# A pre-norm attention and feed-forward block on one Trainium2 core: a different hand-fixed order for the same 1,426 entries

## The chip, the cores and the metric

The kernel runs on one core of one Trainium2 chip. The metric is device microseconds of one execution. Six parts of the core matter: TensorE (PE, with its weight loads shown as PEld), VectorE (DVE), ScalarE (ACT), GpSimd (POOL), SyncE (SP), whose queue issues most of the DMAs, and the DMA engines that carry them.

## The reference

One block with two halves and residual additions. Every operand is bfloat16, with 2,048 tokens, width 640, 32 heads of 20 and a hidden width of 1,728.

```
h  = x + A(layernorm(x))          h2 = h + B(layernorm(h))

A: q, k, v = x @ wq, x @ wk, x @ wv
   for each of 4 segments of 512 tokens:
       a_dot = softmax(q k^T / sqrt(20) + causal mask) v          (within the segment)
       a_mem = (phi(q) M) / (phi(q) z + 1e-6)                     (memory of earlier segments)
       out   = sigmoid(beta) * a_mem + (1 - sigmoid(beta)) * a_dot
       M, z += phi(k)^T v, sum phi(k)       phi(t) = t + 1 if t > 0 else exp(t)
   A = out @ wo
B: silu(x @ w1) @ w2
```

## The kernel before

The program is cut into named tasks, and a list called `ORDER` (line 356) puts every one of them in a row. An entry is `name/engine:slots`. The letter after the slash picks the engine where a task may run on more than one: A is ScalarE, D VectorE, G GpSimd, and S the SyncE queue. The numbers are the buffers that the task takes, for most of them one of the eight PSUM banks. `schedule` (line 287) walks the list once, fixes engine and buffers of each task, and every engine then gets its instructions in the order of the list. A tracker adds the semaphore waits that the buffers need. So an engine never overtakes: an instruction that waits holds all that stands behind it on that engine, DMA issues among them.

The work of a segment `s` of four blocks of 128 tokens, with the lines that the profile names:

- `n1_st`, `n1_r`, `n1_ap`: statistics (L743, L746), reciprocal root (L754 to L764) and scaling (L770) of the first layer norm. `n1_tr` transposes a block by DMA into `xT` (L799); the four blocks of segment 0 go through TensorE instead (`n1_tp`, L779; `n1_te`, L791, L792). `n2_` is the same for the second norm, into `hT`.
- `re_wq`, `re_wk` (L693, L695): the weights of the queries and keys are rearranged once.
- `v` (L828) and `ve` (L842, L843): values, and their eviction from PSUM.
- `pr` (L867, L872) and `qe` (ScalarE L883 or VectorE L884): queries and keys of a chunk of heads, and the eviction. In segment 0 each is cut into token halves x and y.
- `ex` (ScalarE, L890), `pha` (L897), `phb` (L903): phi of queries and keys.
- `vt` (L915) and `vp` (L928): DMAs that copy the heads which don't fit into the first five groups from one place of SBUF to another, twelve for each segment. Groups 5 to 7 of the scores can't start before all twelve `vt` have landed.
- `qk` (TensorE, L965) makes the scores of a group of four heads in four PSUM banks, `e` (ScalarE, L977) takes their exponential, either for four banks at once (a `+` in the name) or for two and two, and `mk` (GpSimd, L988) masks a diagonal block.
- `av` (L1009, L1093), `oe` (L1022, L1024, L1111), `tn` (L1039, L1043, L1124), `nm` (L1057 to L1063, L1136, L1138), `ad` (L1071): attention output, transposed back, normalised and added to the part from the memory.
- `kt`, `kg`, `kh`, `mz`, `ma`, `mb`: the memory of the next segment (transpose L1208, gather L1199, matmul L1226, sums L1238 to L1250).
- `ot` (DMA transpose, L1265), `wo` (L1273), `rs` (L1281): output projection and first residual.
- `h1` (L1302, L1308), `th` (ScalarE tanh, L1317), `s` (L1323), `h2` (L1350), `o` (L1363), `out` (L1368): the feed-forward half and the store. The last block's `h2` and `o` are cut into columns of 320, 192 and 128.
- `zf0` (L649) and `lsc` (L638 on) are small constants made from beta; `fill` (L620) are matmuls on zeros that keep TensorE busy: thirty at the start and two at the end of the list.

Segments overlap freely: the first half of one stands among the second half of the segment before it.

Of the kernel before, what the change touches and what calls it, by code (L numbers as in the profile page):

```python
# [370 lines left out]
e0ya+:4 w_w1_2 ve12/D av4x:4 oe4x/D:0 mz00:5 ma00/A:2,5 qk1ya0:0 e1ya2:0 tn2x:6 nm2x:0 av6x:7 oe6x/D:1 e1ya0 tn4x:6
nm4x:1 qk2ya0:2 kvz e2ya2:1 tn6x:7 mm3 nm6x:2 n1_tr4 v10:0 n1_st11:2 e2ya0 qk0y20:4 e0y2+:6 w_w1_3 w_w1_1 mk0y2_0
kg00/G:0 mk0y2_256 n1_tr7 v13:2 n1_r11/G qk3ya0:4 e3ya0:3 ve10/D n1_st9:6 n1_r9/D pha041:2 ex031:2 mm6 ve13/D ot1:0
wo1:0 n1_st8:3 e3ya2 ot0 ex011:0 wo0:2 rs1 n2_st1:0 mk0y1_384 w_w1_4 phb011 qk4ya0:4 e4ya0:2 n2_r1/D kg02/G e4ya2 rs0
# [11 lines left out]
mz02:6 pha101:1 vt13/S mk8b_384 th0_0_0:0 e9b2 mk9a_0 mk9b_0 mk8e_256 h1_0_9_0:7 th0_9_0:1 s0_0_0 ma02/D:0,4,6,7
qk10a0:0 e10a0:3 mzc2 h1_0_13_0:6 h2_0_0:4 e10a2 w_w2_4 ot3 h2_0_1 mk9b_384 mk10a_0 phb101 n1_r10/D pha111:2 vt19/S
mzc0 mb00:0,0 w_w2_3/S s0_9_0 n1_ap11:2 pha100:0 phb100 th0_13_0:0 s0_13_0 ex131:0 phb131 pha110:0 n1_ap10:1 vt12/S
qk10b0:0 e10b+:6 epsg1 av8:7 oe8/D:0 n1_tr8:0 av9:6 oe9/D:1 n1_tr9 ex110:0 phb110 vt18/S vt110/S h2_0_2 mk10b_0
mk10b_384 qk10e0:0 e10e2:2 e10e0 n1_tr11 h2_0_3 ex121:0 h2_1_0:6 o0 kt13:0 qk11a0:2 pha121:0 phb121 wo3:0 rs3 n2_st3:3  # L390
mk10e_0 mk10e_256 h2_1_1 e11a+:4 mk11a_0 vt14/S qk11b0:2 kg13/G:0 ex130:1 tn8:0 e11b+:5 h2_1_2 vt11/S h2_1_3 pha140:0
nm8:1,1 o1 kh13/G n2_r3/G ex111:2 phb111 mm1 n2_ap3:2 mk11b_0 mk11b_384 pha130:0 vt16/S mzc1 vt111/S ot2 qk12a0:2
e12a+:0 ex140:0 mzc3 mb01:0,0 wo2:0 rs2 av10:7 oe10/D:0 phb140 ad8:0 qk12b0:2 e12b0:3 mzc5 kt12:1 mz10:0 ma10 e12b2
mk12b_0 kg12/D n1_tr10 pr220:6 phb130 vt15/S vt17/S qk13a0:0 e13a+:1 mk13a_0 qe220/D:0 vp13/S:0 tn9:4 vp19/S v20:6
nm9:2,0 ve20/D:0 kt11:0 qk12e0:0 e12e+:6 vp18/S av11:4 n2_st2:4 v21:6 n2_r2/D qk13b0:0 vp15/S oe11/D:1 pr211:5 e13b+:4
# [10 lines left out]
ot4 pr230:5 pha240:0 phb210 qe230/D v22:6 ve22/D ex230:0 ot5 out1/S h1_0_13_1:4 th0_13_1:0 qk17b0:0 e17b2:3
h1_0_11_1:5 th0_11_1:1 vt29/S pha231:1 phb231 phb211 e17b0 wo6:6 mk16e_256 s0_13_1 s0_11_1 qk18b0:2 e18b2:6 mk17b_0
e18b0 mk18b_0 rs6 n2_st6:3 ex220:2 av16:0 oe16/D:1 wo7:6 rs7 n2_r6/D qk17a0:2 wo4:0 vt28/S e17a+:0 h1_0_9_1:7
th0_9_1:0 ex240:1 kg10/G vt27/S n2_st7:0 mk18b_384 vt21/S mk17b_384 vt211/S h1_0_3_1:6 mk17a_0 rs4 th0_3_1:1 n2_st4:2
s0_9_1 qk18e0:2 e18e0:1 n2_r4/D wo5:0 s0_3_1 vt23/S h1_0_2_1:7 e18e2 mk18e_0 phb240 rs5 th0_2_1:0 s0_2_1 h1_0_1_1:6  # L410
th0_1_1:1 vt24/S s0_1_1 qk18a0:2 e18a0:2 vt25/S av17:1 oe17/A:0 kt23:1 x12/S h2_2_0:6 h2_2_1 n2_ap6:1 n2_st5:6
n2_tr6:0 n2_r7/G mk18e_256 n2_ap7:3 n2_tr7 phb220 vt22/S e18a2 qk19b0:0 pha230:0 phb230 vp21/S:0 e19b0:4 tn17:4
nm17:3,1 n2_ap4:1 n2_tr4 pha200:0 h2_2_2 e19b2 h2_2_3 mk18a_0 n2_r5/G qk19a0:0 h2_3_0:4 h2_3_1 e19a2:0 o2 ad17:0
vp22/S e19a0 n2_ap5:3 n2_tr5 out2/S mk19a_0 vp24/S ex200:0 kh14/D av18:6 oe18/D:0 vt210/A phb200 qk20b0:0 e20b+:3
h2_3_2 mk19b_0 h2_3_3 o3 vp25/S ex201:1 kg14/G mz12:7 mb10:0,0 tn18:1 nm18:3,0 mk19b_384 av19:0 h1_1_10_0:6 oe19/A:0
# [1011 lines left out]
```

## Time and profile before

| | |
|---|---|
| median of 3 runs | 296.61 us (296.48 to 296.85) |
| span of the profiled execution | 296.3 us |
| TensorE, matmuls | 282.1 us busy, 2,968 in the profile |
| VectorE | 222.2 us busy |
| ScalarE | 217.3 us busy |
| GpSimd | 140.0 us busy |
| granted TensorE clock | 1.000 over the whole span |

The page of the profile has one row for each engine, the span in 40 slices, the DMA queues, the chain of work that ended last, and the costliest groups of instructions. Busy time of TensorE has the fill and drain of its pipeline in it, so a short wait can hide inside it. A row of a group tells the number of instructions, their busy time together, the mean of one in ns, and the idle time of the engine just before them with what ended it. A row of the timeline tells start, length, engine, line, what is written and read, and in brackets the idle time before it.

### The profile page before, as it was taken

The page shows a single profiled execution, that of the slowest core. Times are in us where ns is not written, and L with a number is a line of the kernel's source. Part 1 is how long each engine was busy: PE and PEld are TensorE (multiplying, and loading weights), DVE is VectorE, ACT ScalarE, POOL GpSimd, SP SyncE. Part 2 cuts the span into 40 slices and gives each one's busy share as a digit, 9 for nine tenths or more (in the row PEclk, how much of TensorE's full clock was granted, in tenths as well). Part 3 has the DMA queues.
Part 4 walks back from the last instruction along what each step waited for, and adds up shares of the span by engine and source line. Part 5 has one row for each costly group of instructions (what it writes and reads, how often), then busy time and mean ns, then how long its engine had stood idle before and what let it go on. Part 6 is the DMA issues. An engine that isn't in the chain of part 4 may idle for free.

```text
span 296.3 us, 7415 instructions
## 1 busy us (share of the span) xinstructions
PE 282.1 (95%) x2968; PEld 167.6 (57%) x2991; DVE 222.2 (75%) x506; ACT 217.3 (73%) x266; POOL 140.0 (47%) x257
## 2 busy tenths in 40 slices
PE   7897889999999999999999999999999999999997
PEld 5675445555665455566643545465665457764575
DVE  3897799778979779899698967759967688626522
ACT  4884989999999899998879999788759750014400
POOL 6237735645566477646526646455476620200000
PEclk9999999999999999999999999999999999999999
DMA  7956973803953221255433400144171023220002
GB/s 243 367 173 105 173 133 71 221 18 75 189 94 74 53 60 22 40 109 106 104 96 61 66 1 2 27 76 87 22 99 32 0 61 74 68 67 25 22 22 91
DMA packets 49922, 25.40 MB, mean 86 GB/s; under 512 B 39504, under 2 KB 48048, under 8 KB 49888
## 3 DMA queue, kind: packets, MB, share of 16 engines
q1 hardware_dynamic: 47804, 22.69, 36.2%
q10 hardware_dynamic: 2084, 2.23, 2.4%
q8 instruction: 24, 0.39, 0.5%
q14 instruction: 10, 0.08, 0.1%
HBM read 10.41 MB, written 2.62 MB: 44 GB/s over the span
## 4 chain that ended last, share of the span: by engine, by line
PE 78%; DVE 8%; DMA 6%; issue 2%; ACT 2%; SPq 1%; POOL 1%; DVEq 0%; ACTq 0%
PE ps_all L1350 19%; PE ps_all L1308 17%; PE ps_all L867 12%; PE ps_all L965 7%; PE ps_all L1273 6%; PE ps_all L828 5%; PE ps_all L1009 5%; DMA x_tok<-in_A_x_dram 3%; DMA xT<-xn_rot 2%; ACT PT L977 2%; PE ps_all L1039 1%; DVE stt L743 1%; PE ps_all L1093 1%; DMA w_sb<-w_sb 1%; PE ps_all L1226 1%
## 5 line engine op out<-in xcount | busy, mean ns | idle before, releaser
L977 ACT ACTIVATE PT<-ps_all 128x1024 bf16<-128x1024 f32 (+1 forms) x120 | 153.2, 1310 | 16.9 <-PE ps_all L965 15.7
L988 POOL TENSOR_SCALAR_AFFINE_SELECT PT<-PT 128x512 bf16<-128x512 bf16 x128 | 81.6, 648 | 59.2 <-ACT PT L977 56.9
L1350 PE MATMUL ps_all<-w_sb,sT 128*128 128x320 bf16 (+2 forms) x462 | 64.9, 295 | 0.0
L1308 PE MATMUL ps_all<-hT,w_sb 128*128 128x512 bf16 (+1 forms) x315 | 61.0, 336 | 1.2 <-issue 0.6
L1317 ACT ACTIVATE th<-ps_all 128x512 f32<-128x512 f32 (+2 forms) x70 | 34.1, 505 | 35.3 <-PE ps_all L1308 31.2
L1350 PEld LDWEIGHTS ps_all<-w_sb,sT 128*128 128x128 bf16 x462 | 43.2, 98 | 18.3 <-issue 1.8
L1323 DVE SCALAR_TENSOR_TENSOR sT<-th,ps_all 128x512 bf16<-128x512 f32 (+2 forms) x70 | 37.9, 561 | 17.8 <-ACT th L1317 16.9
L1308 PEld LDWEIGHTS ps_all<-hT,w_sb 128*128 128x128 bf16 x325 | 29.9, 98 | 25.3 <-issue 3.5
L764 POOL TENSOR_TENSOR rst<-rst,eps_c 128x1 f32<-128x1 f32 x32 | 18.3, 576 | 24.4 <-DVE rst L758 23.1
L743 DVE BATCH_NORM_STATS2 stt<-x_tok 128x6 f32<-128x320 bf16 x62 | 27.2, 481 | 1.1 <-DMA x_tok<-in_A_x_dram 0.7
L1363 DVE SCALAR_TENSOR_TENSOR x_tok<-ps_all,x_tok 128x640 bf16<-128x640 f32 (+3 forms) x18 | 13.3, 745 | 16.7 <-PE ps_all L1350 16.6
L1071 POOL TENSOR_TENSOR otok<-on 128x320 bf16<-128x320 bf16 x24 | 19.0, 797 | 11.7 <-DVE on L1063 11.7
L1273 PE MATMUL ps_all<-wo_sb,oT 128*128 128x320 bf16 x160 | 23.8, 299 | 0.0
L884 DVE CAST QK<-ps_all 128x512 bf16<-128x512 f32 x23 | 15.7, 688 | 9.1 <-PE ps_all L867 8.9
L1063 DVE TENSOR_TENSOR on<-ps_all,rd 128x640 bf16<-128x640 f32 x24 | 19.8, 824 | 0.9
L828 PE MATMUL ps_all<-wv_sb,xT 128*128 128x320 bf16 x120 | 18.3, 299 | 1.1 <-DMA xT<-xn_rot 0.9
L1273 PEld LDWEIGHTS ps_all<-wo_sb,oT 128*128 128x128 bf16 x160 | 15.0, 98 | 7.2 <-issue 1.8
L867 PE MATMUL ps_all<-xT,wkr 128*128 128x512 bf16 x67 | 16.9, 379 | 1.2 <-issue 0.8
L867 PE MATMUL ps_all<-xT,wqr 128*128 128x512 bf16 x70 | 17.3, 380 | 0.4 <-issue 0.2
L1009 PE MATMUL ps_all<-PT,Vx 128*32 128x512 bf16 (+3 forms) x384 | 16.4, 301 | 0.1
L843 DVE CAST Vx<-ps_all 128x640 bf16<-128x640 f32 x15 | 12.3, 818 | 5.4 <-PE ps_all L828 5.3
L770 DVE TENSOR_SCALAR xn_rot<-x_tok,mvt,rst 128x640 bf16<-128x640 bf16 x32 | 14.9, 475 | 1.7 <-POOL rst L764 1.0
(106 smaller groups left out, 337.4 us busy)
## 6 DMA issues: line engine op xcount, KB each, us to landing
w_sb<-in_B_w_dram SPq DMA_DIRECT2D x5, 432.0 KB, 6.3
w_sb<-in_B_w_dram SPq DMA_DIRECT2D x3, 480.0 KB, 4.6
x_tok<-in_A_x_dram SPq DMA_DIRECT2D x2, 640.0 KB, 9.7
out_dram<-x_tok ACTq DMA_DIRECT2D x8, 160.0 KB, 1.8
out_dram<-x_tok SPq DMA_DIRECT2D x7, 160.0 KB, 1.9
x_tok<-in_A_x_dram SPq DMA_DIRECT2D x3, 320.0 KB, 3.4
QKV<-QK SPq DMA_DIRECT2D x12, 72.0 KB
wo_sb<-in_A_wo_dram SPq DMA_DIRECT2D x1, 800.0 KB, 10.4
```

The lines of the kernel that those rows point to most:

```text
L743: T.add(DV, lambda e, hh=hh: e.bn_stats(out=stt[:, s, 6 * hh:6 * hh + 6], in_=xb[:, 320 * hh:320 * hh + 320]), reads=R((xa, xsub)), writes ...
L828: fns.append(lambda e, c=c, hh=hh: e.matmul(bank(ps, hh)[:, 0:320], lhsT=xT_[:, c, 128 * i:128 * i + 128], rhs=wv_sb[:, c, 320 * hh:320 * ...
L867: fns = [lambda e, kc=kc: e.matmul(bank(ps)[:, lo:hi], lhsT=wt[:, kc, c, :], rhs=xT_[:, kc, lo:hi], start=(kc == 0), stop=(kc == NC - 1)) ...
L965: fns.append(lambda e, j=j, o=o, r=r, q0=q0, q1=q1, qa=qa, ka=ka: e.matmul(ps_all[:, o:o + q1 - q0], lhsT=ka[32 * r:32 * r + DH, 128 * j:1 ...
L977: T.add(AC, lambda e: e.activation(out=pt[:, pta.slot, q0:q0 + nq, 0:width], in_=sc3[:, b0:b0 + nq, 0:width], func=ACT.Exp, scale=SCALE), ...
L988: T.add(PO, lambda e: e.affine_select(out=v, in_=v, pattern=[[0, 4], [1, 128]], compare_op=ALU.is_ge, fill=0.0, base=0, channel_multiplier ...
L1009: fns.append(lambda e, j=j, r=r, h=h, pa=pa, pt=pt, co=co, q0=q0, ji=ji: e.matmul(bank(po)[32 * r:32 * r + 32, q0:hi], lhsT=Vx[:, vx.slot, ...
L1273: fns.append(lambda e, c=c, hh=hh: e.matmul(bank(ps, hh)[:, 0:320], lhsT=oT[:, c, 128 * i:128 * i + 128], rhs=wo_sb[:, c, 320 * hh:320 * h ...
L1308: fns = [lambda e, c=c: e.matmul(bank(ps)[:, lo:hi], lhsT=w1_sb[:, c, 128 * f:128 * f + 128], rhs=hT[:, c, lo:hi], start=(c == 0), stop=(c ...
L1317: T.add(AC, lambda e: e.activation(out=th[:, tha.slot, lo:hi], in_=bank(ps)[:, lo:hi], func=ACT.Tanh, scale=0.5), reads=R((ps, [0])), writ ...
L1323: T.add(DV, lambda e: e.scalar_tensor_tensor(out=sT[:, f, lo:hi], in0=th[:, tha.slot, lo:hi], scalar=1.0, in1=bank(ps)[:, lo:hi], op0=ALU. ...
L1350: fns.append(lambda e, f=f, t0=t0, fr=fr, hh=hh, n=n: e.matmul(bank(pa, hh)[:, 0:n], lhsT=sT[:, f, t0:t0 + 128], rhs=w2_sb[:, fr, c0 + 320 ...
```

## The change

Only the list is another one. The 1,426 names are the same, and so are the tasks themselves and the sizes of the buffers. What differs is the order from the second line on, the PSUM banks and other slots, and the engine of some tasks that have a choice:

- 12 tasks go from VectorE to ScalarE (`re_wq1`, `qe000y`, `qe001y`, `qe010y`, `qe011y`, `ve01`, `oe11`, `qe211`, `qe301`, `qe330`, `ve33`, `oe26`), and 6 the other way (`qe041y`, `qe101`, `qe200`, `qe310`, `qe320`, `oe22`).
- 29 DMAs go from the SyncE queue to ScalarE's, among them 13 `vt` and 11 `vp`, and 13 go back. ScalarE issues 37 DMAs instead of 21.
- Sixteen small tasks (`n1_r`, `n2_r`, `kg`, `kh`) go from VectorE to GpSimd and nine the other way.
- The two `fill` matmuls stand in the middle of segment 3 (before `tn24`) instead of behind the last matmul.
- In the last block the columns are finished in another order: 128, 320, 192 instead of 320, 192, 128.

Of the diff, the lines that matter below:

```
-re_wq1/D:0 pr010x:4 re_wq4/A re_wq2/D pr020x:2 qe020x/A:0 qe010x/A:0 re_wq3/D re_wq0/D pr000x:5 pr040x:6 w_k1
...
-qe040y/A vt02/S:0 vt011/S vt05/S vt08/S n1_st5:1 qk0x30:0 vt04/S mk0x1_0 mk0x1_256 n1_st4:5 n1_r5/G n1_ap5:1 e0x3+:0
-n1_ap6:2 pr000y:4 qe000y/D lsc0 vt07/A pr021y:6 qe021y/D pr001y:5 qe001y/D pr011y:7 ex021:0 qe011y/D pr020y:1 n1_r4/D
-mk0x3_0 qe020y/D mk0x3_256 vt010/A pr010y:6 qe010y/D vt00/A vt03/A vt06/S v03:2 ve03/D:0 ex001:1 mk0x3_384 mk0x2_0
-v00:4 ve00/D qk0y10:0 e0y12:5 mk0x1_384 pha021:1 pha001:2 v01:6 e0y10 mk0y1_0 mk0x2_256 vt09/S phb021 vt01/S qk4x10:2
...
-n2_ap1:0 n2_st0:0 pr101:0 qe101/A:0 av0y:1 qk0y30:2 e0y3+:0 w_w2_0/S pr120:6 zf0 n2_r0/D oe0y/D:0 pr100:7 mk0y3_0
+re_wq1/A:0 re_wq0/D w_k1 x2:0,2 pr000x:4 re_wq4/A re_wq2/D pr020x:6 mm3 qe020x/A:0 re_wk2/A:0 w_wv0:0 re_wq3/D
...
+mk0x1_0 zf0 lsc0 qe030y/D zf1 qk0x30:0 e0x3+:0 pr021y:7 qe021y/D x8/S:7,8,11,9 vt011/A:0 pr000y:6 pr020y:5 n1_st5:5
+vt02/S mm2 pr001y:7 qe001y/A vt05/S mk0x1_256 qe020y/D n1_st7:4 n1_r7/G pha001:1 pr011y:0 lsc1 lsc2 pr010y:4 v03:2
+qe011y/A qe010y/A qe000y/A qk0y10:4 n1_ap7:1 v00:0 vt01/A vt03/A ve03/D:1 ex001:1 v01:2 phb001 mm1 e0y10:1 n1_r5/G
+n1_ap5:3 ve00/D vt06/A mk0x3_0 vt010/S n1_st4:4 n1_r6/G mk0x2_256 mk0x3_256 vt07/S vt04/S n1_ap6:2 v02:0 ve02/D vt00/A
+vt08/S ex021:0 e0y12 pha021:2 phb021 ve01/A mk0x1_384 mk0x3_384 ex011:2 vt09/S qk4x20:4 av2x:2 e4x2+:2 mk4x2_0
...
+e4ya0:5 e4ya2 mzc6 n2_st0:2 n2_r0/G mzc3 pr101:1 qe101/D:0 av0y:0 oe0y/D:1 qk0y30:2 pr100:6 n2_ap1:0 qe100/D e0y3+:3
...
+h2_5_0:6 vt35/S e27b2 mk26e_0 n2_st9:4 n2_r9/G kt21:1 mz21:1 ma21 mb21:0,0 kg22/D fill2:0 tn24:4 nm24:1,1 n2_st11:7
...
-h2_15_1_1 h2_15_2_1 h2_15_0_2:3 h2_15_3_1 out15_0/A o15_1 h2_15_1_2 h2_15_2_2 h2_15_3_2 o15_2 out15_2/A out15_1/S
-fill2:2
+o15_2 h2_15_1_0 h2_15_2_0 h2_15_3_0 o15_0 h2_15_0_1:5 out15_2/S h2_15_1_1 h2_15_2_1 out8/S h2_15_3_1 o15_1 out14/A
+out15_1/S out15_0/A
```

More of the change, by code (lines that the diff above doesn't have):

```diff
@@ L371 @@
[L371 to L374, printed above, removed]
-n2_ap1:0 n2_st0:0 pr101:0 qe101/A:0 av0y:1 qk0y30:2 e0y3+:0 w_w2_0/S pr120:6 zf0 n2_r0/D oe0y/D:0 pr100:7 mk0y3_0
@@ L386 @@
[L386 to L395, printed above, removed]
@@ L406 @@
[L406 to L415, printed above, removed]
```

158 lines of the change are left out of this document (90 added, 68 removed).

## The prediction

> **What bounds the kernel now.** I read the page's first part, then busy time by stage, then the waits, then the chain and the timeline where the waits point.
>
> ```profile
> PE 282.1 (95%) x2968; PEld 167.6 (57%) x2991; DVE 222.2 (75%) x506; ACT 217.3 (73%) x266; POOL 140.0 (47%) x257
> ```
>
> Over the whole span TensorE (PE) looks like the only bound. By stage it is not; the columns are the length, then PE, PEld, DVE, ACT and POOL, busy us with the instructions in brackets.
>
> ```profile
> 20.00:30.00 10.00, 8.50 (x86) 6.19 (x84) 8.22 (x20) 5.40 (x7) 5.69 (x11) 1.00 0.53 93
> 30.00:45.00 15.00, 12.63 (x195) 7.20 (x194) 12.95 (x31) 13.25 (x13) 9.28 (x17) 1.00 0.86 149
> 45.00:80.00 35.00, 33.40 (x441) 19.77 (x444) 29.45 (x76) 34.55 (x46) 19.03 (x35) 1.00 0.51 115
> 80.00:145.00 65.00, 63.93 (x724) 37.23 (x731) 56.31 (x129) 59.69 (x71) 40.17 (x72) 1.00 0.38 73
> 145.00:240.00 95.00, 93.07 (x987) 49.86 (x994) 72.22 (x151) 78.27 (x85) 53.04 (x88) 1.00 0.28 49
> ```
>
> From 20 to 45 us nobody is full: TensorE idles 1.50 + 2.37 us and ScalarE 4.60 + 1.75, each waiting for the other or for data. From 45 to 80 ScalarE is the bound (0.45 us idle in 35). From 80 on TensorE is (1.07 us idle in 65, 1.93 in 95), with ScalarE 5.3 us short of full in the 65. So a new order can win in the first 80 us and can only win small waits, or lose, behind that. How the two engines hand time to each other stands in the waits:
>
> ```profile
> ACT PT L977 <- PE ps_all L965: 15.7, 28, 1.8
> PEld ps_all L965 <- ACT PT L977: 13.2, 33, 1.8
> PE ps_all L965 <- DMA w_sb<-w_sb: 1.5, 1, 1.5
> PE ps_all L828 <- DMA xT<-xn_rot: 0.9, 1, 0.9
> ```
>
> The exponentials wait for scores, and the scores for banks that exponentials must empty. Two single waits of TensorE are for landings, and the chain of work that ended last runs through both:
>
> ```profile
> 24.60 3.73 DMA w_sb<-w_sb
> ...
> 35.73 6.91 DMA xT<-xn_rot
> ```
>
> The first is the last of the twelve `vt` copies of segment 0, the second the last transposed block of segment 1 (`n1_tr7`).
>
> **The change part by part.** The tasks are the same, so TensorE's work is the same; what can differ is its waiting, and what ScalarE, where it is full, has to do. I cost the change against the profiled execution (span 296.3 us, 0.3 below the median of 296.61) and carry the difference over to the median.
>
> *The first wait.* TensorE and ScalarE around the `vt` landing:
>
> ```profile
> 22.29 2.88 PE L828 MATMUL ps_all<-wv_sb,hT 128*128 128x320 bf16 x20
> 25.11 0.40 PE L965 MATMUL ps_all<-w_sb 20*128 20x256 bf16 x12
> 25.44 1.53 PE L828 MATMUL ps_all<-wv_sb,hT 128*128 128x320 bf16 x10
> 28.47 0.40 PE L965 MATMUL ps_all<-w_sb 20*128 20x256 bf16 x12 [1.50 <-DMA w_sb<-w_sb]
> ```
>
> ```profile
> 21.36 3.34 ACTq L915 DMA_DIRECT2D w_sb<-w_sb  x3
> 25.56 1.94 ACT L977 ACTIVATE PT<-ps_all 128x1024 bf16<-128x1024 f32 x2 [0.18 <-PE ps_all L965]
> 28.92 1.88 ACT L977 ACTIVATE PT<-ps_all 128x2048 bf16<-128x2048 f32 x1 [1.43 <-PE ps_all L965]
> ```
>
> Before, TensorE has three of the four value blocks done when it starts to wait at 26.97 and goes on at 28.47. In the new list the fourth (`v02`, half of the 2.88, so 1.4) stands ahead of the wait: it arrives at 28.4, plus 0.2 that I give to a later start of the y halves (block 2's scaling now stands behind block 3's), 28.6. Equal progress before is 28.47 + 1.4 = 29.9. When does the last copy land? Seven now go on SyncE's queue and five on ScalarE's, and ScalarE also takes the four y evictions.
>
> ```profile
> L883 ACT ACTIVATE w_sb<-ps_all 128x256 bf16<-128x256 f32 x11 | 3.7, 388 | 0.9 <-PE ps_all L867 0.9
> L890 ACT ACTIVATE ex<-w_sb 128x512 bf16<-128x512 bf16 x5 | 3.1, 626 | 3.0 <-DVE Vx L843 2.8 <-DVE w_sb L884 0.2
> L883 ACT ACTIVATE QK<-ps_all 128x512 bf16<-128x512 f32 x7 | 4.2, 600 | 0.1
> L649 ACT ACTIVATE zf<-beta_bc 128x32 f32<-128x32 bf16 x1 | 0.2, 222 | 0.0
> L915 ACTq DMA_DIRECT2D w_sb<-w_sb x4: 701/860/1617, 19.2 to 23.8; - x4
> out_dram<-x_tok ACTq DMA_DIRECT2D x8, 160.0 KB, 1.8
> ```
>
> The last y projection drains some 0.2 us after the first value block begins, so at 22.29 + 0.2, and with the 0.2 of the later start at 22.7. Behind it on ScalarE stand two evictions (0.39 each, 23.5), two issues (0.86 each, the first beside an eviction, 24.8), `ex001` (0.63, 25.4), then `e0y10` with two issues beside and behind it: the last starts at 26.3. Every one of these waits holds what is behind it, above all `ex021` and `e0y12`; they are needed only by matmuls behind the same landing. From issue to landing the chain shows 3.73 us for such a copy; the shortest row near it is a store's 1.8. That gives 28.1 to 30.0. I take 29.2, between the two, because the DMA engines are only 0.53 busy in 20:30 and five copies start on another queue: first scores at 29.2, 0.7 better than 29.9, range 1.3 better to 0.1 worse.
>
> For ScalarE the first four-bank exponential then starts at 29.2 + 0.45 = 29.65 instead of 28.92, 0.73 later, but with `ex011` (0.63) already behind it, which before stood among the full stretch. (`ex021`, `e0y12`, the eviction `ve01`, which ScalarE takes over, and `ex011` fill its time from the last issue on; if they run longer than to 29.65, the start is late by up to 0.3 more, which is in the range.) It also gets time back at the second landing:
>
> ```profile
> 41.88 1.88 ACT L977 ACTIVATE PT<-ps_all 128x2048 bf16<-128x2048 f32 x1 [0.21 <-PE ps_all L965]
> 44.59 1.02 ACT L977 ACTIVATE PT<-ps_all 128x1024 bf16<-128x1024 f32 x1 [0.84 <-PE ps_all L965]
> ```
>
> `n1_tr7` is issued behind fewer weight loads in the new list, so `v13` no longer holds the scores of group 3. They still need the banks of the exponential at 41.88, so of the 0.84 only about 0.4 goes, and the 0.21 goes too; `ex041` (0.63) fills what is left, 0.2 over. Sum at that point: +0.73 - 0.63 - 0.4 - 0.2 + 0.2 = **-0.3**, range -1.0 to +0.8.
>
> [...]
>
> *The full stretch, 45 to 80.* The order of exponentials is the same; of other work ScalarE loses `qe101` (0.60) and `zf0` (0.22, now ahead of 20 us, where it idles). With 0.45 us idle in 35 all of it counts: **-0.8**. VectorE takes `qe101` and has 5.5 us of room in that stretch; if VectorE's order is late there instead, the term is 0. The three `vt` issued on ScalarE here stand behind exponentials and cost nothing, as these rows show: the issue runs beside the exponential, and the next one starts on time.
>
> ```profile
> 143.02 1.02 ACT L977 ACTIVATE PT<-ps_all 128x1024 bf16<-128x1024 f32 x1 [0.70 <-PE ps_all L965]
> 143.03 0.75 ACTq L915 DMA_DIRECT2D QKV<-QK  x1
> 143.94 1.02 ACT L977 ACTIVATE PT<-ps_all 128x1024 bf16<-128x1024 f32 x1
> ```
>
> *80 to 145.* Here ScalarE issues fourteen copies and stores that SyncE issued before.
>
> ```profile
> L915 ACTq DMA_DIRECT2D QKV<-QK x2: 716/732/747, 143.0 to 190.4; - x2
> L928 ACTq DMA_DIRECT2D phiQv<-phiQ x3: 642/677/801, 217.3 to 221.7; - x3
> ```
>
> Singles behind an exponential are free. Four pairs are not: `vt110`, `vt111` behind an `ex` (2 x 0.73 - 0.63 = 0.83), `vp15`, `vp111` behind an eviction (2 x 0.68 - 0.60 = 0.75), `vt27`, `vt29` and `vt22`, `vt21` behind a two-bank exponential (2 x 0.73 - 1.02 = 0.44 each): 2.5 us in which the next exponential can't start. One eviction more (two come, one goes; 0.60) makes 3.1. ScalarE has 5.3 us idle here and is not the bound, so I put 0.3 on the path; the ends are 0 and 3.1. On the other side, SyncE's queue loses some 10 of these issues at 0.7 us each and its transposes get out earlier; TensorE's 1.07 us idle bounds that gain, I take 0.1. Together **+0.2**, range -1.1 to +3.1.
>
> *The rest.*
>
> ```profile
> L620 PE MATMUL ps_all<-zpad 128*128 128x256 bf16 x32 | 5.2, 333 | 1.1 <-DVE zpad L597 1.1
> 293.44 0.36 DVE L1363 SCALAR_TENSOR_TENSOR x_tok<-ps_all,x_tok 128x192 bf16<-128x192 f32 x1 [0.89 <-PE ps_all L1350]
> 293.80 0.38 PE L620 MATMUL ps_all<-zpad 128*128 128x256 bf16 x2
> 294.00 0.29 DVE L1363 SCALAR_TENSOR_TENSOR x_tok<-ps_all,x_tok 128x128 bf16<-128x128 f32 x1 [0.20 <-PE ps_all L1350]
> ```
>
> The two zero matmuls ran beside the last addition, for nothing; now they stand among TensorE's full stretch: at most 0.33, I take **+0.2**. The last piece is 192 columns instead of 128: 0.36 - 0.29 = +0.1. The order of the last `h1` can give as much back; 0. From 145 to 240 ScalarE has 16.7 us idle, which hides the four evictions it gains (it loses three): 0.
>
> *Tasks between VectorE and GpSimd.* Sixteen go one way, nine the other. What two engines' closeness costs can be seen at phi:
>
> ```profile
> L897 DVE TENSOR_SCALAR phiQ<-QK 128x512 bf16<-128x512 bf16 x15 | 5.6, 381 | 0.0
> L897 DVE TENSOR_SCALAR phiQ<-QK x15: 240/285/879, 56.3 to 205.3; 128x512 bf16<-128x512 bf16 x15
> ```
>
> The mean is 96 ns above the median, 1.4 us over fifteen instructions, all of it on an engine with 8.7 us of room in 80:145: 0 in the sum. [...]
>
> Sum: -0.3 - 0.8 + 0.2 + 0.2 = **-0.7 us**, so 295.9.
>
> **The rivals.** *More is won.* TensorE's idle time from 30 to 80 is 2.37 + 1.60 us, and its short waits for banks are hidden in busy time. If the new banks take half of that (2.0) in addition, 0.7 + 2.0 = 2.7: 293.9. For it: the waits between L965 and L977 are 61 short ones, the kind that an order decides. Against: ScalarE is full in most of it.
>
> *Nothing moves.* The copies land as late as before (+0.5 instead of -0.3) and the rest holds: -0.7 + 0.8 = +0.1, 296.7.
>
> *ScalarE's queue becomes the bound.* If the four pairs (2.5) fall where TensorE waits for the next scores' banks, the 0.3 becomes 2.5: -0.7 + 2.2 = +1.5, 298.1. It decides from about 1.0 us of unhidden issue on. For it: 92% of 80:145 is already busy on ScalarE. Against: TensorE is 98% busy there, so ScalarE works ahead of need.
>
> **How the numbers follow.** A measurement of this kernel can tell about 0.2%, 0.6 us, from no change. Forecast 0.33, more is won 0.20, nothing moves 0.20, ScalarE's queue 0.27. The forecast lies just over the line and the case above it well over: faster 0.52, same 0.20, slower 0.28. The range takes in 293.9 and 298.1 and a little of the bounds outside: 293.7 to 298.3. The forecast's own range, with its first term at either end, is 295.2 to 297.0.
>
> **What would show it.** Right: `L965 <- DMA w_sb<-w_sb` under 1 us or gone, `L828 <- DMA xT<-xn_rot` gone, the 0.84 us before the exponential near 44 us halved, and the scores of group 10 about a microsecond earlier than before. Wrong: issues of L915 and L928 on ScalarE's queue with the next L977 idle behind them and TensorE's L965 waiting for that; or a first exponential behind the landing later than 30.4.

## The result, and the profile after

The list after is slower: 305.73 us median of 4 runs (305.58 to 307.18) against 296.59 us (296.48 to 296.85), a ratio of 1.0313 with a 95% interval of 1.0287 to 1.0340. The forecast was 295.9 with a range of 293.7 to 298.3, so it was wrong in sign and in size. The profiled execution took 305.58 us with a span of 303.9. Its first page has a first sign in the line of the clock, one digit of which is not a 9 (slice 9, 60.8 to 68.4 us):

```profile
PEclk9999999959999999999999999999999999999999
```

The same stages as in the prediction; of the two numbers behind the instruction counts the first is the granted clock, the second the share of the DMA engines:

```profile
20.00:30.00 10.00, 9.47 (x103) 6.77 (x105) 8.70 (x23) 7.45 (x12) 6.86 (x16) 1.00 0.49 81
30.00:45.00 15.00, 11.13 (x188) 6.62 (x176) 11.68 (x26) 13.33 (x12) 10.80 (x18) 1.00 0.45 97
45.00:80.00 35.00, 30.49 (x370) 17.25 (x369) 23.66 (x58) 27.70 (x34) 14.01 (x28) 0.90 0.49 127
80.00:145.00 65.00, 63.20 (x748) 37.28 (x750) 54.60 (x126) 60.45 (x73) 40.16 (x75) 1.00 0.43 67
145.00:240.00 95.00, 93.16 (x982) 50.97 (x988) 71.88 (x156) 81.49 (x90) 53.20 (x92) 1.00 0.34 60
```

The loss sits in 45:80, where ScalarE was to win 0.8 us: TensorE is busy 30.49 us instead of 33.40 at a clock of 0.90, and ScalarE 27.70 instead of 34.55. From the waits of the two engines:

```profile
ACT PT L977 <- PE ps_all L965: 16.0, 31, 0.9
PE ps_all L1308 <- DMA hT<-xn_rot: 3.4, 1, 3.4
PE ps_all L965 <- DMA QKV<-QK: 0.8, 1, 0.8
```

One wait is new and long: the first product of the feed-forward half (`h1`, L1308) waits 3.4 us for `hT`, the transposed second norm. The DMA issues and the product around it, from the timeline, and how long the transpose issued at 54.68 (`n2_tr0`) took, from the answer on its line:

```profile
52.12 1.21 SPq L799 DMA_TRANSPOSE hT<-xn_rot  x1
53.37 1.26 SPq L1208 DMA_TRANSPOSE phiKt<-phiK  x1
54.68 1.28 SPq L799 DMA_TRANSPOSE hT<-xn_rot  x1
55.12 0.42 ACTq L582 DMA_DIRECT2D w_sb<-in_B_w_dram  x1
56.00 1.27 SPq L1208 DMA_TRANSPOSE phiKt<-phiK  x1
61.33 2.32 PE L1308 MATMUL ps_all<-hT,w_sb 128*128 128x256 bf16 x10 [3.39 <-DMA hT<-xn_rot]
```

```profile
L799 SPq DMA_TRANSPOSE hT<-xn_rot x1: 1277/1277/1277, 54.7 to 54.7; - x1
...
DMA to landing us min/median/max: 6.6/6.6/6.6
```

The transposes issued at 52.12 and 53.37 landed after 2.6 and 2.5 us. `n2_tr0`, third of the train, with the 640 KB load `w_w2_0` issued 0.44 us behind it on the other queue, took 6.6. And behind the wait the clock halves:

```profile
53.73:57.15 3.42, 2.93 (x59) 1.57 (x59) 2.97 (x7) 3.42 (x5) 1.15 (x2) 1.00 0.69 125
57.15:60.56 3.41, 0.78 (x4) 0.17 (x2) 0.69 (x1) 1.83 (x2) 1.91 (x3) 1.00 1.20 220
60.56:63.97 3.41, 2.64 (x18) 1.48 (x18) 0.42 (x1) 0.68 (x2) 0.00 (x0) 0.50 0.44 144
63.97:67.39 3.42, 3.42 (x26) 2.50 (x22) 2.14 (x7) 2.35 (x3) 0.00 (x0) 0.50 0.00 0
```

Two stretches of 3.41 us at exactly half clock follow one in which TensorE was busy for 0.78 us. My theory at this point: the late landing costs 3.4 us, the half clock it brings some 2.9 more, and all else about what was forecast. The rivals: the transpose is late because of its own place on the queue and not because of the load; the clock falls for another reason; ScalarE's 16 more DMA issues are what costs.

### The profile page after: what moved, and what is told of

Its sections match the earlier page's. It is cut to its first block, busy times and chain, and to the rows that moved or that the text cites. A ratio compares the mean times of both kernels' runs of the same rounds, so it can differ in the third digit from the quotient of the medians.

```text
span 303.9 us, 7408 instructions
## 1 busy us (share of the span) xinstructions
PE 285.1 (94%) x2968; PEld 169.9 (56%) x2991; DVE 218.1 (72%) x492; ACT 220.2 (72%) x273; POOL 140.5 (46%) x264
## 4 chain that ended last, share of the span: by engine, by line
PE 73%; ACT 9%; DMA 7%; DVE 6%; issue 2%; SPq 1%; POOL 1%; ACTq 1%; DVEq 0%
PE ps_all L1350 19%; PE ps_all L1308 16%; PE ps_all L867 12%; PE ps_all L965 7%; PE ps_all L1273 7%; ACT PT L977 7%; PE ps_all L1009 4%; PE ps_all L828 3%; DMA hT<-xn_rot 2%; PE ps_all L1039 1%; DMA oT<-otok 1%; DMA w_sb<-w_sb 1%; DVE stt L743 1%; DMA QKV<-QK 1%; PE ps_all L1043 1%
## 5 line engine op out<-in xcount | busy, mean ns | idle before, releaser
L988 POOL TENSOR_SCALAR_AFFINE_SELECT PT<-PT 128x512 bf16<-128x512 bf16 x128 | 81.0, 647 | 62.9 <-ACT PT L977 60.8
L1308 PE MATMUL ps_all<-hT,w_sb 128*128 128x512 bf16 (+1 forms) x316 | 62.8, 346 | 4.3 <-DMA hT<-xn_rot 3.4
L1308 PEld LDWEIGHTS ps_all<-hT,w_sb 128*128 128x128 bf16 x325 | 31.0, 101 | 30.0 <-DMA hT<-xn_rot 3.9
L884 DVE CAST QK<-ps_all 128x512 bf16<-128x512 f32 x24 | 16.4, 684 | 5.9 <-PE ps_all L867 5.6
L770 DVE TENSOR_SCALAR xn_rot<-x_tok,mvt,rst 128x640 bf16<-128x640 bf16 x32 | 17.0, 535 | 2.5 <-POOL rst L764 2.5
L1281 DVE TENSOR_TENSOR x_tok<-ps_all,x_tok 128x640 bf16<-128x640 f32 x16 | 13.1, 817 | 5.0 <-PE ps_all L1273 4.9
```

What stands on the lines that cost most here:

```text
L988: T.add(PO, lambda e: e.affine_select(out=v, in_=v, pattern=[[0, 4], [1, 128]], compare_op=ALU.is_ge, fill=0.0, base=0, channel_multiplier ...
L1308: fns = [lambda e, c=c: e.matmul(bank(ps)[:, lo:hi], lhsT=w1_sb[:, c, 128 * f:128 * f + 128], rhs=hT[:, c, lo:hi], start=(c == 0), stop=(c ...
```

## The experiments

All are edits of the list alone; seven of them add matmuls on zeros. Ratios are against the list before on the same chip. "Lag" is how much later a task starts on TensorE than in the second trace of the list before (next paragraph). Times to landing and waits are each from the one trace of a list.

**The base of comparison (`b0`).** The list before, unchanged.

> The list before, unchanged, for a second trace of it. In the runs so far time minus span is 1.7 to 1.8 us for every list, but 0.3 for the profiled execution of before against its median (296.6 and 296.3). Theory: that profiled execution was a long one of some 298 us; a new trace shows a span of 294.9 to 295.5, and where the 1 to 1.4 us lay. Rival: the span is again 296.3.

It took 296.93 us with a span of 295.2, and its trace has no wait for `xT`. Time minus span is 1.7 to 1.9 for every run of every list here. So the profiled execution of before that the prediction was worked out from was a long one (by the same 1.7 some 298.0 us); 0.34 us of its surplus lay at the wait for `xT` near 44 us. Against this second trace the lag of after grows as these rows show, first before, then after, the same tasks (scores of five stages):

```profile
46.39 0.40 PE L965 MATMUL ps_all<-w_sb 20*128 20x256 bf16 x8
54.74 0.40 PE L965 MATMUL ps_all<-w_sb 20*128 20x256 bf16 x8
59.90 0.40 PE L965 MATMUL ps_all<-w_sb 20*128 20x256 bf16 x8
118.98 0.40 PE L965 MATMUL ps_all<-QK 20*128 20x512 bf16 x4
231.37 0.40 PE L965 MATMUL ps_all<-QKV 20*128 20x512 bf16 x4
```

```profile
48.00 0.40 PE L965 MATMUL ps_all<-w_sb 20*128 20x256 bf16 x8
56.35 0.40 PE L965 MATMUL ps_all<-w_sb 20*128 20x256 bf16 x8 [0.24 <-ACT PT L977]
67.74 0.40 PE L965 MATMUL ps_all<-w_sb 20*128 20x256 bf16 x8
125.99 0.39 PE L965 MATMUL ps_all<-QK 20*128 20x512 bf16 x4
239.72 0.39 PE L965 MATMUL ps_all<-QKV 20*128 20x512 bf16 x4
```

+1.6 by 46 us, nothing more to 55, +6.2 to 60, -0.8 to 119, +1.3 to 231, and +0.3 to the end: 8.7, the difference of the spans.

**Only the load away (`e1`).**

```
-... e4y12 w_w2_0/A n2_tr0 ... qk4y20:2 e4y2+:4 ...
+... e4y12 n2_tr0 ... qk4y20:2 e4y2+:4 w_w2_0/A ...
```

> The list after, with one entry moved: the 640 KB load of w_w2_0 is issued on ScalarE's queue behind e4y2+ (some 15 us later) instead of behind e4y12; n2_tr0 is issued at about 54.7 us as before this edit. Theory (the load, issued 0.4 us behind n2_tr0, takes the DMA engines from it; TensorE idles 3.4 us for hT; the granted clock then halves for some 7 us and costs 2.9 more): n2_tr0 lands 2.6 to 4.0 us after its issue instead of 6.6, the wait of L1308 for hT is under 0.8 us, the clock stays at 1.0 in 60:70, and the time falls from 305.7 to about 299.7 (299 to 300.5). Rival 1 (the transpose is slow by itself, or because it is issued late, behind kt01): landing and wait stay, 305.7. Rival 2 (the clock falls for another reason than the idle time): the wait goes and the clock still halves, about 302.6.

1.0165 (1.0110 to 1.0220). The wait falls to 1.2 us, the transpose takes 4.4, not 2.6 to 4.0. But the time scatters with the clock: 307.38 at 0.945, 303.39 and 303.01 at 0.989, and 300.43, alone within the expected 299 to 300.5, at 1.0. In the profiled run it fell not near 60 but twice earlier:

```profile
28.89:32.30 3.41, 1.69 (x57) 1.10 (x57) 2.82 (x6) 2.14 (x2) 0.93 (x2) 1.00 0.57 117
32.30:35.71 3.41, 3.41 (x27) 1.72 (x26) 1.21 (x3) 1.88 (x1) 3.19 (x8) 0.50 0.49 95
...
39.13:42.54 3.41, 2.25 (x44) 1.28 (x45) 2.62 (x8) 3.11 (x5) 3.26 (x6) 1.00 0.54 153
42.54:45.95 3.41, 3.41 (x21) 1.56 (x19) 2.39 (x5) 2.07 (x3) 1.50 (x2) 0.50 0.36 70
```

So the part of the list ahead of 45 us, the same as in after, can halve the clock too: behind 3.41 us in which TensorE was busy 1.69, and behind 3.41 with 2.25.

**The transpose earlier (`e2`).**

```
-... n2_ap1:0 qe100/D ... phb041 qe120/D:0 n2_ap0:2 ... qe121/D kt01:1 e4y12 w_w2_0/A n2_tr0 ...
+... n2_ap1:0 n2_ap0:2 qe100/D ... phb041 qe120/D:0 ... qe121/D n2_tr0 kt01:1 e4y12 w_w2_0/A ...
```

> The list after, with n2_ap0 on VectorE moved ahead of qe100, phb041 and qe120, and n2_tr0 on SyncE's queue moved ahead of kt01; w_w2_0 stays behind e4y12 on ScalarE's queue. n2_tr0 should be issued at 53.4 us instead of 54.7. Theory (what counts is that the load comes right behind the transpose): with 1.7 us of lead instead of 0.4 most of the transpose is done when the load begins: it lands at 57.5 to 58.5, the wait is under 0.8 us, 299.7. Rival (the load behind takes the engines however the lead): landing about 1.3 us earlier, a wait of about 2 us, and the clock falls if 2 us are enough for that: 301.5 to 304.4.

300.67 us, 1.0107 (1.0073 to 1.0141), clock 1.0 in every run. `n2_tr0`, second of the train at 53.6, lands after 2.7 us and nobody waits; `kt01`, now third with the load 0.44 us behind it, takes the 6.0 instead, and TensorE waits 0.4 us for it near 61 us. The list is now 3.7 us over before instead of 9.1. What is left shows another landing further on: `PE ps_all L965 <- DMA QKV<-QK: 1.6, 1, 1.6`, the copies `vt2` near 152 us.

**Zeros in the wait (`e3`, `e12`).** `e3` puts 26 zero matmuls ahead of `h1_0_12_0`; `e12` also 8, 5 and 5 ahead of `qk4x10`, `qk1ya0`, `qk2ya0`.

```
-... av0x:3 qk4x10:4 ... av4x:6 qk1ya0:0 ... e1ya0 qk2ya0:2 ... qe141/D:0 h1_0_12_0:7 ...
+... av0x:3 fill8:1 qk4x10:4 ... av4x:6 fill5:7 qk1ya0:0 ... e1ya0 fill5:7 qk2ya0:2 ... qe141/D:0 fill26:7 h1_0_12_0:7 ...
```

> The list after, with 26 more matmuls on zeros for TensorE right ahead of h1_0_12_0, where it waits for hT; nothing of the computation is changed. By the 0.11 us that five 128x256 matmuls take each at full clock they fill some 2.9 of the 3.4 us. Theory (the clock halves because TensorE idles): the wait remains but the clock stays at 1.0 in 60:70, so that the 2.9 us of half clock go and the 3.4 us stay: about 302.8. Rival (the clock falls by itself, or the matmuls come late): no gain or a loss, 305.7 to 306.5.

308.09 us (1.0364, 1.0328 to 1.0400), no gain. The profiled run has a clock of 0.95 over its span of 306.9 us, which I can't explain: at 308.68 us it stands among the others (307.38 to 309.22), with 0.983 to 0.989. It settles little by itself, hence `e12`:

> The list after, with 8, 5 and 5 matmuls on zeros ahead of qk4x10, qk1ya0 and qk2ya0 and 26 ahead of h1_0_12_0, where TensorE waits for hT; nothing of the computation is changed. Theory (after loses 3.3 us to the wait for hT and, in most of its runs, two stretches of 3.4 us at half clock, 3.4 us, that follow from it): n2_tr0 still lands 6 us and more after its issue, the clock is 1.0, and the time is 302.2 to 302.9, a ratio of 1.017 to 1.021. Rival 1 (the half clock is not due to idle time): 305.5 to 306. Rival 2 (the half clock hides nothing, the wait alone costs the whole 6 us): 305.5 with a clock of 1.0.

304.52 us (1.0221, 1.0173 to 1.0270), clock 1.0 in every run. The transpose still takes 6.6 us (6.55), but the clock stays up behind it:

```profile
58.00:60.00 2.00, 2.00 (x20) 1.79 (x19) 0.69 (x1) 1.04 (x1) 1.27 (x2) 1.00 1.60 258
60.00:62.00 2.00, 1.50 (x15) 1.09 (x12) 0.00 (x0) 0.00 (x0) 0.00 (x0) 1.00 0.72 228
62.00:64.00 2.00, 2.00 (x26) 1.44 (x23) 1.37 (x4) 1.75 (x3) 0.00 (x0) 1.00 0.07 25
```

The lag of `qk4y20` is 5.0 us instead of 7.8: the half clock costs 2.8 and the wait the rest of the 6.2, as the theory said, and with TensorE's idle time filled it is gone (1.0 in four runs, against 0.983 to 0.989 in after). In the span only 0.8 of the 2.8 is left; between 87 and 155 us `e12` waits 2.4 us for `oT` (two landings) and 1.0 for `QKV`, where after has 0.9 and 0.8. The expected 302.2 to 302.9 was missed by that.

**The end (`e4`).** `fill2` back behind the last entry.

> The list after, with the two zero matmuls moved from segment 3 back behind the last entry, as in the list before. In the list after the device time is 1.7 us over the span of the profile, in the list before 0.3. Theory A (what is new outside the span comes from the end of the program, where TensorE's last matmuls stood): time minus span goes back to about 0.3, 304.3 or less. Theory B (it comes from the stores at the end, of which SyncE issues five in the last 3 us): time minus span stays at 1.7; the time falls by at most 0.2 for the two matmuls taken from TensorE's full stretch, 305.5 to 305.7.

307.51 us (1.0318, 1.0264 to 1.0373), time minus span 1.7 to 1.9. Both theories fall with `b0`: there was nothing to explain. Nor does the move gain anything that can be measured (1.0318 against 1.0313 for after).

**The copies of segment 2 earlier (`e5`), and zeros against the clock (`e10`).** `e5` is `e2` with this; `e10` is `e5` with the fillers 8, 5 and 5.

```
-... x12/S ... n2_tr5 ... vt210/S ... vt211/S out2/S ... vt25/S vt20/S ...
+... vt20/S vt25/S vt211/S vt210/S x12/S ... n2_tr5 ... out2/S ...
```

> The list with n2_ap0 and n2_tr0 earlier (the run above, 300.67 us, 1.0107 of before), and in addition the last four copies of segment 2 on SyncE's queue (vt210, vt211, vt25, vt20) moved ahead of x12 and the four n2_tr, which they stood behind. Theory (a second landing costs: TensorE waits 1.6 us for these copies near 152 us, where its lag behind the list before grows from 1.2 to 2.6 us): the wait of L965 for QKV is under 0.3 us and the ratio falls to 1.0055 to 1.0075 (298.9 to 299.4 us). Rival (another wait takes its place, for the bank of an exponential or for the n2_tr that are now later): 300.2 to 300.8.

The wait for `QKV` is gone, yet the ratio is 1.0147 (1.0130 to 1.0164): every run has a clock of 0.989 or 0.994, though up to 135 us the list is that of `e2`, where none had.

> The list with n2_ap0, n2_tr0 and the four vt2 earlier (301.35 us, 1.0147 of before, granted clock 0.989 to 0.994: one or two stretches of 3.4 us at half clock in every run, the profiled one at 41.5 us), and in addition 8, 5 and 5 matmuls on zeros for TensorE right ahead of qk4x10, qk1ya0 and qk2ya0, where it waits for exponentials; nothing of the computation is changed. Theory (the clock halves behind a stretch of 3.4 us in which TensorE is busy for less than two thirds; here 0.50 at 28.6 to 32 and 0.61 at 37.6 to 41): the clock is 1.0 in every run and the ratio 1.0065 to 1.0085 (298.9 to 299.5 us). Rival (the clock falls for another reason, or the fillers hold the scores up): 0.989 to 0.994 as before, 301 to 302.

299.44 us (1.0064, 1.0041 to 1.0087), clock 0.999 or 1.0 in all five runs. First `e5`, then `e10`:

```profile
37.00:41.00 4.00, 2.63 (x64) 1.54 (x64) 2.98 (x8) 3.70 (x4) 3.78 (x6) 1.00 0.57 153
41.00:43.00 2.00, 1.98 (x12) 1.28 (x13) 1.74 (x6) 1.96 (x3) 2.00 (x3) 0.63 0.01 5
```

```profile
37.00:41.00 4.00, 3.87 (x77) 2.31 (x75) 2.89 (x7) 3.70 (x5) 3.78 (x7) 1.00 0.59 156
41.00:43.00 2.00, 2.00 (x23) 1.15 (x21) 1.83 (x6) 1.79 (x3) 1.95 (x2) 1.00 0.00 0
```

Eighteen matmuls that compute nothing make the list some 2 us faster (301.35 and 299.44; by the two ratios 2.5). ScalarE's work in 37:41 is the same 3.70; only TensorE's idle time is filled.

**ScalarE's queue (`e7`).** `e2` with all nineteen `vt1`, `vp1`, `vt2`, `vp2` of ScalarE's queue back on SyncE's (`/A` to `/S`).

> The list with n2_ap0 and n2_tr0 earlier (300.67 us, 1.0107 of before), and in addition all nineteen copies vt1, vp1, vt2 and vp2 that ScalarE issues go on SyncE's queue, at the same places of the list. Theory (their issue on ScalarE lies beside other work): within 0.5 us, a ratio of 1.009 to 1.0125. Rival 1 (ScalarE's queue is what costs in 80:240): 1.5 to 2.5 us less, 1.002 to 1.006. Rival 2 (SyncE's queue is short of time, and what ScalarE took over was of use): 1 to 3 us more.

309.85 us (1.0438, 1.0404 to 1.0473). Rival 2, by far more than its 1 to 3 us: SyncE's queue is late, TensorE waits 4.0 us for `QKV` near 157 us, and the clock is 0.978 to 0.989. ScalarE's issues are of use.

**qe101 (`e11`).** `e10` with `qe101/A`.

> The list of the run with the 8, 5 and 5 fillers, with qe101 back on ScalarE as in the list before. The forecast put 0.6 us of its term of -0.8 on taking qe101 from ScalarE, as ScalarE is full from 45 to 80. The trace of after shows TensorE's lag constant from 45 to 57. Theory now (TensorE, with two blocks of the output projection ahead of the scores, sets the pace there, and ScalarE waits for scores ahead of its exponentials): within 0.2 us of that run. Rival (the forecast's term is right and is lost by something else): 0.5 to 0.7 us slower.

299.02 us (1.0061, 1.0040 to 1.0081). Within the intervals the same as `e10`; nine of its ten runs lie between 298.75 and 299.19, all five of `e10` between 299.30 and 299.92, so if anything 0.4 faster. (The tenth, 300.76, is the profiled one, with 2.4 us of waiting for the `vt` copies instead of 0.4.) In its trace the lag doesn't grow from `qk7ya0` to `qk4y20`; in that of `e10` it grows from 1.5 to 2.4, over a wait for `kt01`:

```profile
61.32 0.46 PE L1226 MATMUL ps_all<-Vx,phiKt 128*128 128x84 bf16 x8 [0.68 <-DMA phiKt<-phiK]
```

In `e10` the load goes out 0.44 us behind `kt01`, which lands after 6.3 us; in `e11`, where ScalarE has `qe101` to do as well, 0.97 us behind it, and `kt01` lands after 4.2 and nobody waits. So the 0.4 may be this wait's, and the two times alone don't price `qe101`. The stretch ahead of it does: from 46 to 57 us the lag moves alike in both traces (1.61 to 1.52, 3.67 to 3.58), so that taking `qe101` from ScalarE gained nothing there.

**The collision in the list before (`e6`, `e9`).** `w_w2_0/A` behind `ex101`, and behind `e5ya2`, instead of `/S` ahead of `n2_tr1`.

> The list before, with one entry moved: the 640 KB load w_w2_0 leaves SyncE's queue ahead of n2_tr1 and is issued on ScalarE's queue behind ex101, about 0.5 us behind n2_tr0. Theory (a load issued right behind a transpose takes the DMA engines from it): n2_tr0, issued at about 51.9 us, takes 6.2 to 6.6 us to land instead of 4.0, n2_tr1 lands in 2.6, TensorE waits 1.0 to 1.4 us for hT near 57 to 58 us, and the time rises by as much, 297.6 to 298.0, more where the clock halves. Rival (the list after loses because its transpose is issued late, the load is harmless): no change, within 0.3 us of before.

297.06 us (0.9998, 0.9987 to 1.0008). It tested something else: the load went out at 49.8, 0.7 us behind `n2_tr1`, which took 4.8 us; both transposes were in time.

> The list before, with w_w2_0 issued on ScalarE's queue behind e5ya2. In the last run it was meant to fall behind n2_tr0 but went out at 49.8 us, while an exponential ran, 0.7 us behind n2_tr1, and both transposes landed in time. Here the issue must wait for the scores of group 5 and so falls at about 52, 0.5 to 1 us behind n2_tr0 (51.4). Theory (the load takes the engines from the transpose it follows): n2_tr0 lands after 6.0 to 6.6 us instead of 4.0, at 57.5 to 58, TensorE needs it at 56.2 and waits 1.3 to 1.8 us; the time is 298.2 to 298.9, more where the clock halves, a ratio of 1.0045 to 1.012. Rival (the transposes of the list before have room whatever follows them, and the list after is late by its own order): within 0.3 us of before.

297.52 us (1.0004, 0.9987 to 1.0021). The load went out at 52.4, 0.9 us behind `n2_tr0` (51.5), which landed after 2.6 us all the same. My theory that a load behind a transpose is enough fell here; I asked what part the place in the train has.

**Place and load apart (`e13`, `e14`), and both in the list before (`e15`).** `e13` and `e14` are after with the fillers 8, 5, 5; `e13` has `kt01` behind `n2_tr0`, `e14` `w_w2_0` behind `e4y2+`; `e15` is before with `kt01` ahead of `n2_tr0` and `w_w2_0/A` behind `e5ya2`.

> The list after with the fillers of 8, 5 and 5 matmuls (so that the clock stays up to 45 us), and on SyncE's queue kt01 moved behind n2_tr0; n2_ap0 and w_w2_0 stay. The transpose n2_tr0 is then the second of the train n2_tr1, n2_tr0, kt01, kt03 instead of the third, issued at about 54.5 us, with the 640 KB load some 0.6 us behind it as in after. Theory A (the load behind the transpose is the cause): it still lands 5.5 us and more after its issue, TensorE waits 2 us and more, 302 to 304.5 (1.018 to 1.026). Theory B (what is slow is the third transpose of a train, and a load behind it makes that worse): it lands in 2.6 to 3 us, the wait is gone, 299.5 to 300.2 (1.0085 to 1.011).

303.51 us (1.0196, 1.0147 to 1.0244): theory A. Second of the train, with the load 0.7 us behind:

```profile
L799 SPq DMA_TRANSPOSE hT<-xn_rot x1: 1202/1202/1202, 54.4 to 54.4; - x1
...
DMA to landing us min/median/max: 5.6/5.6/5.6
```

> The list after with the fillers of 8, 5 and 5 matmuls and w_w2_0 issued some 15 us later, behind e4y2+; n2_tr0 stays third in the train behind kt01. In the run without fillers it landed after 4.4 us, with a clock that had fallen elsewhere. Theory A (the load is the whole cause): 2.6 to 3 us to landing, no wait, 299.5 to 300.2. Theory B (both: third place and the load): 4.0 to 4.6 us, at 58.7 to 59.3, a wait of 0.8 to 1.4 us, 300.3 to 301.3 (1.0115 to 1.0145).

300.94 us (1.0118, 1.0070 to 1.0165), clock 1.0 in every run: theory B. Third of the train, without the load, and a wait of 1.08 us:

```profile
L799 SPq DMA_TRANSPOSE hT<-xn_rot x1: 1276/1276/1276, 54.8 to 54.8; - x1
...
DMA to landing us min/median/max: 4.3/4.3/4.3
```

Both count, then: 2.6 and 2.7 as second of the train with the load 0.9 and 1.7 us behind (`e9`, `e2`), 4.3 by the place, 5.6 by the load 0.7 us behind, 6.6 by both. In these traces the load counts by how close it follows: `kt01`, where it is third, takes 6.0 and 6.3 us with the load 0.44 us behind (`e2`, `e10`), but 4.2 and 4.1 with it 0.97 us behind (`e11`, `e16`), no more than `n2_tr0` without it. How a load and a transpose come to hold each other up, and why the third place costs, no run here shows.

> The list before with the two things that after has: kt01 ahead of n2_tr0 on SyncE's queue, so that n2_tr0 is third of the train, and w_w2_0 on ScalarE's queue behind e5ya2, where it went out at 52.4 us. n2_tr0 is issued at about 51.7. Both theories that name the place in the train and the load together (B): it lands after 6.0 to 6.6 us, at 57.7 to 58.3, TensorE needs it at 56.2 and waits 1.5 to 2.1 us, 298.4 to 299.2 (1.005 to 1.0075), more where the clock halves. Rival (the list before has room for this): within 0.3 us of before.

297.46 us (1.0011, 0.9986 to 1.0037): the rival. The transpose, issued at 52.0, did take 5.5 us, but the wait was 0.4. The list before issues it so early that even this landing (57.5) comes within half a microsecond of need (57.2 in this run). The loss of after takes the late issue as well.

**The start (`e16`).** `e11` with `pr030x` behind the first scores and `vt00` on SyncE's queue.

> The fastest list so far (n2_ap0, n2_tr0 and the vt2 earlier, fillers, qe101 on ScalarE; 299.0 us, 1.0061 of before) with two things of the start put back: pr030x behind the first scores instead of ahead of them, and the copy vt00 on SyncE's queue behind vt08 instead of last on ScalarE's. Theory (of the 2.1 us that this list still loses 1.6 lie ahead of 45 us: 1.0 because seven instead of six projections stand ahead of the first scores and because of the loads, the rest because the last copy lands at 29.3 instead of 27.9): the first scores come 0.5 us earlier, the scores of group 4 0.6 to 1.0 us earlier, and the time is 298.0 to 298.5 (1.0035 to 1.005). Rival (the start isn't on the path, as ScalarE waits for values anyway): no change, 298.8 to 299.2.

300.04 us (1.0094, 1.0062 to 1.0127): missed. The first scores come 0.7 us earlier than in `e11`, but the last copy, now issued at 25.0 instead of 25.8, landed near 29.7, 4.6 us later (3.7 in after), and TensorE waits 1.0 us for it. The waits for `oT` near 131 and 133 are 1.9 us together, against 1.0 in `e11`. The 1.6 us of lag come from the landing and not from the projection: the scores behind it start at 27.90 in `b0`, 29.36 in after, 29.72 here and 31.41 in the trace of `e11`, and the lag at 46 us is 1.61, 1.98 and 3.67, each time that start's delay and some 0.15. What sets the landing of these copies (3.6 us in `e10` to 5.6 in `e11`) stays open.

None of these lists beats the list before, and the three edits of it (`e6`, `e9`, `e15`) measure the same as it; the best repair of after is `e11`.

## Why the prediction was wrong

**The step that failed** is the one on "the full stretch, 45 to 80". It read the stretch from ScalarE's share (34.55 of 35), took `qe101` and `zf0` off it for -0.8, and allowed at worst 0 "if VectorE's order is late there instead". It summed engines, and didn't follow what stands behind `qe101` on VectorE, in which order SyncE issues the transposes then, and where the load moved to ScalarE's queue goes out. That chain is in the list: `qe101`, two other evictions and `phb041` ahead of `n2_ap0`, `kt01` ahead of `n2_tr0`, `w_w2_0` right beside it. VectorE in after:

```profile
50.51 0.64 DVE L884 CAST QK<-ps_all 128x512 bf16<-128x512 f32 x1
...
52.02 0.69 DVE L884 CAST QK<-ps_all 128x512 bf16<-128x512 f32 x1
52.62 0.42 DVE L903 TENSOR_TENSOR phiK<-phiK,ex 128x512 bf16<-128x512 bf16 x1
53.10 0.69 DVE L884 CAST QK<-ps_all 128x512 bf16<-128x512 f32 x1
53.70 0.71 DVE L770 TENSOR_SCALAR xn_rot<-x_tok,mvt,rst 128x640 bf16<-128x640 bf16 x1
```

In the second trace of before the same scaling (L770) runs from 50.49 to 50.94: 3.5 us earlier at its end, of which the general lag is 1.6. The transpose was issued at 54.68 instead of 50.96 and took 6.6 instead of 4.0 us; TensorE needed it at 57.94. Measured: +6.2 instead of -0.8. With that scaling and that transpose alone moved ahead (`e2`), 5.5 of the 9.1 us are back.

**The clock** was in no term. Where it fell it read 0.50, for 3.41 us (`e4`; `e1`, twice) or 6.83 (after). By an estimate from this length each 3.41 us costs up to 1.7; `e12` showed 2.8 for the 6.83 of after. Whether it falls differs between runs of one list: the clock over the span is 0.989 in two runs of `e1` and 1.0 in one. In the 3.41 us ahead of a fall TensorE was busy for 0.78 (after), 1.69 and 2.25 (`e1`) by the records, so it did not stand idle all that time. Busy time alone doesn't tell when the clock falls either: in `e4` it stayed at 1.00 behind 3.42 us with 2.03, and fell behind the next, with 1.38. What sets it off, no run here shows.

```profile
55.45:58.87 3.42, 2.03 (x40) 0.90 (x29) 1.91 (x3) 3.42 (x3) 1.51 (x3) 1.00 0.94 144
58.87:62.28 3.41, 1.38 (x18) 1.01 (x18) 0.21 (x1) 0.51 (x3) 0.39 (x1) 1.00 0.90 283
62.28:65.69 3.41, 3.41 (x29) 2.44 (x22) 2.27 (x8) 2.57 (x3) 0.00 (x0) 0.50 0.00 0
```

**The second queue.** The first term counted on an earlier landing for copies that start on ScalarE's queue. The last copy took 3.74 us from there, and 3.73 from SyncE's in the profile of before. The case "nothing moves" had kept those 3.73: 26.3 + 3.73 is 30.0, 0.8 behind 29.2, and so +0.5 for the term instead of -0.3. A load on ScalarE's queue and a transpose on SyncE's were in no term: the transpose takes 5.6 us with the load 0.7 us behind (`e13`), 2.6 with it 0.9 us behind (`e9`).

**The first wait.** Landing forecast 29.2, measured 29.3, and that is luck: the last copy was issued at 25.57 and not 26.3, and took 3.74 us and not the 2.9 that 29.2 leaves; the two errors cancel. Scores at 29.36 (0.53 us of wait, under the 1 us named); first four-bank exponential at 29.80 for 29.65, so 0.88 later than before for 0.73; the wait for `xT` gone. The sum was -0.3 (range to +0.8). Against the execution that it was made from, the lag at 44.9 us is +0.70; against the second trace it is +1.6. So of the 1.03 us that the term took off for `ex011` and the second landing, 0.2 came. `ex011`, done ahead, freed nothing that shows, as the exponentials wait for scores as before (16.0 us in 31 waits; 15.7 in 28 before). Nor did the fourth value block, done ahead of the wait: in `b0` it runs from 28.23 to 29.76 beside the first four-bank exponential, whose banks the next scores need anyway. In after:

```profile
29.80 1.88 ACT L977 ACTIVATE PT<-ps_all 128x2048 bf16<-128x2048 f32 x1 [0.75 <-PE ps_all L965]
31.74 0.40 PE L965 MATMUL ps_all<-w_sb 20*128 20x256 bf16 x12 [1.21 <-ACT PT L977]
32.25 1.88 ACT L977 ACTIVATE PT<-ps_all 128x2048 bf16<-128x2048 f32 x1 [0.57 <-PE ps_all L965]
...
45.18 2.89 PE L1273 MATMUL ps_all<-wo_sb,oT 128*128 128x320 bf16 x20
48.00 0.40 PE L965 MATMUL ps_all<-w_sb 20*128 20x256 bf16 x8
```

The two engines take turns from 29 us on. Near 45, two blocks of the output projection (2.89 us) stand on TensorE ahead of the scores, so time that ScalarE saves there is waited out. That fits why -0.8 did not come even ahead of the late transpose: the lag is +1.61 at 46.39 and +1.61 at 54.74, and it moves as little in `e11`, where `qe101` is back on ScalarE.

**80 to 145.** +0.2 forecast (-1.1 to +3.1); the lag falls by 0.8 from 60 to 119 us. The rival "ScalarE's queue becomes the bound" was wrong: `e7`, with the copies back on SyncE's queue, is 3.3% slower than `e2` by the two ratios. **The rest:** +0.2 forecast, for the two zero matmuls (`e4` shows no gain from taking them back) and the last piece; the lag grows by 1.3 to 231 us, of it some by the `vt2` copies (0.8 us of wait in after; 1.6 in `e2`, none in `e5`), and 0.3 at the end.

**VectorE and GpSimd.** The 0 for the tasks that change between them was worked out from phi, and no run prices it. In the profile of before a 128 x 512 phi on VectorE takes 0.28 and 0.29 us with no GpSimd instruction beside it (56.27, 76.37). The long ones each have one beside them (0.67 at 92.17, 0.88 at 142.50), but so do some of 0.28 (85.01, 186.88). What makes the difference, the traces don't show.

**The rivals** had the path still running through ScalarE or the first landing. Of the four cases with a chance of their own, none had a landing that the change itself makes late.

## What to carry to other kernels

When a list is reordered, follow each transposed or copied tile from its producer's place on its engine, through the place of its DMA on its queue, to what is issued within a microsecond of it on any queue (here a load 0.44 and 0.7 us behind a transpose counted), and compare its landing with the time of need; a table of busy shares shows none of this. Ask of a wait on TensorE not only how long it is but also what the granted clock does behind it: here it fell to 0.50 behind 3.41 us with TensorE busy for 0.78 to 2.25. A few matmuls on zeros where it waits anyway were a cheap guard here (18 of them, some 2 us, `e10` against `e5`). Before a forecast, compare the profiled execution's own time, not its span, with the median: one trace can be a microsecond off.

## What was not expected of the hardware

- A DMA transpose of 128 x 640 lands 2.6 to 2.7 us after its issue as first or second of a train with no load just ahead or less than 0.9 us behind it, 4.3 and 4.4 (`e14`, `e1`) as third of a train of transposes 1.3 us apart, 5.6 as second (`e13`) and 4.8 as first (`e6`) with a 640 KB load 0.7 us behind it, and 6.2 to 6.6 with both (four runs, 6.6 in after and `e12`; 5.5 in `e15`); with the load 0.9 us behind it (`e9`) 2.6. Where the load stood ahead of it, in the list before, 4.6 as first and 4.0 as second (`b0`).
- The granted clock fell to 0.50 for 3.41 us (`e1`, `e4`) or 6.83 (after), also behind stretches of 3.41 us in which TensorE was busy for 1.69 and 2.25 (`e1`), and differently in different runs of the same list (1.0 to 0.989 over the span in `e1`).
- In one profiled run (`e3`) the granted clock was 0.95 over the span, at 308.68 us among runs of 307.38 to 309.22 with 0.983 to 0.989; no run here shows why.
